# Decode attention on one core: uneven first output weights, one store semaphore, a split last weight load and smaller last value pieces

## The chip, the cores and the metric

The kernel runs on one core of a Trainium2 chip. The metric is the device time of one execution in microseconds (us). Three runs of the kernel before gave 1368.85, 1369.17 and 1373.74, a median of 1369.17 us.

## The reference

Two attention layers decode one token each for a batch of 4, and their outputs stand side by side.

```python
q = (x @ wq).reshape(B, Sq, Hq, Dh).transpose(0, 2, 1, 3)
scores = einsum("bhqd,bhkd->bhqk", q, k) * Dh ** -0.5
p = softmax(scores)
o = einsum("bhqk,bhkd->bhqd", p, v)
return o.transpose(0, 2, 1, 3).reshape(B, Sq, Hq * Dh) @ wo
```

Layer A has 32 query heads on 8 key heads and looks at the last 2048 of 8192 positions. Layer B has 32 heads with keys and values of their own over all 8192 positions. A head has 128 elements, a token 512; all arrays are bfloat16. The caches of B alone are 2 x 268 MB, and each byte is used once: nearly all of the work is reading.

## The kernel before, in words

**Chunks.** The work is cut into 40 chunks. Eight belong to A (one key head, all four batch rows; 2 MB of keys, 2 MB of values), 32 to B (four heads of one batch row; 8.39 MB of keys and as much of values). In SBUF each of the 128 partitions holds a row of consecutive positions, so that a load has 128 long rows.

**Queues.** SP issues all loads but the two small ones of x, in a fixed order (lines 468 to 489): A's weights, A's chunks with A's output weights (`dma_wo`, line 359) between them, then for B, before every fourth chunk, 512 rows of output weights (`dma_wos`, line 367), and for each chunk its keys (`dma_kB`, line 388) and its values (`dma_vB`, line 438). The last two loads of A's output weights (LATEWO = 2) come at the very end, behind B's last values. Each issue waits on semaphores for the moment at which its place in SBUF is free; as a rule that is some us before the queue has run dry.

**Pieces.** A chunk of B comes whole, or near the beginning and the end in pieces: the list in line 32 (LASTV) gives those of the last value chunk in tiles of 128 positions, of which a chunk has 256. GpSimd waits for each piece and passes its arrival on by raising a semaphore (`land_vB`, line 452, `land_wos`, line 461; emitted at line 82), in groups of eight tiles; the list QV in line 35 says before which groups TensorE waits.

**Compute.** TensorE transposes the keys (line 571), multiplies them with the query (line 613), and multiplies values with probabilities (`emit_pv`, line 747). It reorders B's output weights with matmuls (`reorder`, line 834), whose first reader of a load stands at the head of a chunk. `emit_fin` (line 852) multiplies a chunk's result with its output weights and adds it into one PSUM tile, `fin`: four products (one for each matrix row of the four that a partition holds) in two halves, which run side by side as a pair.

**The end.** After the last chunk's `emit_fin` TensorE ends B's sum (line 1041), does A's chunk 6, then waits for the last output weights and does A's chunk 7. `emit_out` (line 872) casts B's and A's sums with VectorE and stores each from ACT and from SP, four rows of 512 bytes each. SP waits for the stores at lines 1051 and 1052.

Every operation passes through a scheduler (`_Sched`, line 60) that gives each keyed operation a semaphore and a count; matmuls are recorded at lines 501 and 503 for all callers.

Of the kernel before, what the change touches and what calls it, by code (L numbers as in the profile page):

```python
# [13 lines left out]
P = 128  # L14
# [3 lines left out]
NH = 10  # L18
NWO = 2
LATEWO = 2  # L20
NPB = 2
NSM = 2
SLAG = 2
# [5 lines left out]
QUARTERS = (64, 64, 64, 64)  # L29
NLATE = 4  # L30
NEXTV = (128, 64, 64)
LASTV = (128, 64, 32, 32)
QK = (0, 4, 8)
QC = (16, 24)
QV = (0, 8, 16, 24, 28)
NBUSY = 2
MOREBUSY = 5
FILL = (6, 3)
# [140 lines left out]
def bass_concat_heads__sliding_block_cached__mha_block_cached__decode_kernel(  # L179
# [6 lines left out]
    DO = A_wo.shape[1]  # L186
# [23 lines left out]
    NCA = Hkv  # L210
# [9 lines left out]
    chunks.append(dict(chunks[NCA]))  # L220
    assert all(sum(x) == NTB for x in (LASTV, NEXTV, ENDK, QUARTERS, HALVES, WHOLE)) and NTA * 16 == 1024 and NTB * 4 == 1024
    NCP = (NTB - KMAIN) // TG

    sch = _Sched()
    with ExitStack() as es:
        block = es.enter_context(nc.Block())

        def sb(name, shape, dt):
            return es.enter_context(nc.sbuf_tensor(name, shape, dt))

        def ps(name, shape, dt):
            return es.enter_context(nc.psum_tensor(name, shape, dt))
# [3 lines left out]
        wos = sb("wos", [P, 4, DO], BF16)  # L236
# [29 lines left out]
        pm = sb("pm", [P, HB, NB, 4], F32)  # L266
        pbt = {0: sb("pba", [P, NPB, NTA * 16 + NW], BF16), 1: sb("pbb", [P, 2, NTB * 2 + NW], BF16)}
        oT = sb("oT", [P, NSM, 16], BF16)
# [12 lines left out]
        fin = ps("fin", [P, 512], F32)  # L281
        xtps = ms[:, XT0:XT0 + KC * NB].bitcast(BF16)
        po2 = tr[:, 2, :].bitcast(F32)

        semnames = ["eng_pe", "eng_dve", "eng_act", "eng_pool", "eng_sp", "d_x0", "d_x1", "d_o0", "d_o1", "r_k", "r_v", "r_c", "r_w"]
        semnames += ["d_h%d" % i for i in range(NH)] + ["d_%s%d_%d" % (f, n, i) for f in "kv" for n in range(1, 6) for i in range(n)]
        semnames += ["d_wo%d" % i for i in range(NWO)] + ["d_wos"]
        sems = {n: es.enter_context(nc.semaphore(n)) for n in semnames}
# [4 lines left out]
            out=identb[:, :], in_=onesb[:, :], pattern=[[1, P]], compare_op=ALU.is_equal,  # L293
# [4 lines left out]
            out=identf[:, :], in_=onesf[:, :], pattern=[[1, P]], compare_op=ALU.is_equal,  # L298
# [3 lines left out]
            out=ind[:, :].rearrange("u (x i) -> u x i", x=4), in_=onesf[0:4, :].rearrange("u (x i) -> u x i", x=4),  # L302
            pattern=[[1, 4], [0, P // 4]], compare_op=ALU.is_equal, fill=0.0, base=0, channel_multiplier=-1),
            waits=["c_onesf", "c_identf"], key="c_ind")
# [14 lines left out]
        for r in range(4):  # L319
            sch.add("pool", lambda e, r=r: e.affine_select(  # L320
                out=sel4[:, r, :], in_=onesb[:, :], pattern=[[0, 4], [-4, 32]], compare_op=ALU.is_equal,
# [4 lines left out]
        for u in range(4):  # L326
            sch.add("pool", lambda e, u=u: e.affine_select(
                out=back[:, :, :], in_=back[:, :, :], pattern=[[1, 4], [-1, P]], compare_op=ALU.not_equal,
# [21 lines left out]
        def dma_wq(ab, at):  # L350

            waits = take(("wq", ab), at, 2, ("qmm", ab))
            src = WQ[ab].rearrange("(p r) n -> p (r n)", r=KC)
            sch.add_dma("sp", lambda e: e.dma_start(flat(at, 2), src), "d_h%d" % at, waits=waits, key=("wq", ab))

        def wo_slot(g):
            return g % 2

        def dma_wo(g):

            src = A_wo[g * 4 * P:(g + 1) * 4 * P, :].rearrange("(p r) n -> p (r n)", r=4)
            slot = wo_slot(g)
            dst = wor[:, slot, :]
            sch.add_dma("sp", lambda e: e.dma_start(dst, src), "d_wo%d" % slot,
                        waits=[("fin", g - 2)] if g >= 2 else [], key=("wo", g))

        def dma_wos(hq):


            src = B_wo[4 * hq * P:4 * (hq + 1) * P, :].rearrange("(p r) n -> p (r n)", r=4)  # L370
            sch.add_dma("sp", lambda e: e.dma_start(wos[:, :, :].rearrange("p r n -> p (r n)"), src), "d_wos",
                        waits=[("reord", NCA + 4 * hq - 1, 3)] if hq else [], key=("wos", hq))

        def dma_A(kind, c):
            ch = chunks[c]
# [9 lines left out]
        def vpieces(c):  # L385
            return LASTV if c == NC - 1 else NEXTV if c == NC - 2 else HALVES if c <= NCA + 2 or c == NC - 3 else WHOLE

# [50 lines left out]
        def dma_vB(c):  # L438

            ch = chunks[c]  # L440
            src = B_v[ch["b"], 4 * ch["hq"]:4 * ch["hq"] + 4].rearrange("u (pp j) d -> (u pp) (j d)", pp=P // 4)
            dst = flat(VB, 4)
            pieces = vpieces(c)
            fam = "d_v%d_" % len(pieces)
            j0 = 0
            for i, n in enumerate(pieces):
                waits = held[4] + held[5] + held[6] + held[7] if c == NCA else [("pv", c - 1, 0 if j0 + n <= NTB // 2 else 1)]
                x = slice(j0 * P, (j0 + n) * P)
                sch.add_dma("sp", lambda e, x=x: e.dma_start(dst[:, x], src[:, x]), fam + str(i), waits=waits, key=("v", c, i))
                j0 += n  # L450

        def land_vB(c):
# [3 lines left out]
            for i, m in enumerate(pieces):  # L456
                sch.relay("pool", sems, "r_v", m // TG, [("v", c, i)])
            for g, end in zip(QV, QV[1:] + (NTB // TG,)):
                sch.tk[("vr", c, g)] = ("r_v", n * (NTB // TG) + end)
# [12 lines left out]
        for c in range(NCA):  # L472
            if c != 1 and c < NCA - 1:
                dma_A("k", c + 1)
            dma_A("v", c)
            if c == 2:
                dma_wq(1, 6)
            if c != 1 and c < NCA - LATEWO:
                dma_wo(c)
            if c == 0:  # L480
                dma_wo(1)
                dma_A("k", 2)
        for c in range(NCA, NC):
# [3 lines left out]
            dma_vB(c)  # L487
        for c in range(NCA - LATEWO, NCA):
            dma_wo(c)
# [9 lines left out]
        def pe_mm(o, l, r, start=True, stop=True, transpose=False, waits=(), key=None):  # L499
            if transpose:  # L500
                sch.add("pe", lambda e: e.transpose(o, l, r), waits, key)  # L501
            else:
                sch.add("pe", lambda e: e.matmul(o, l, r, start=start, stop=stop), waits, key)  # L503
# [223 lines left out]
        def spread_A(c, bs):  # L727

            for b in bs:
                sch.add("act", lambda e, b=b: e.activation(  # L730
                    probs_of(c).rearrange("p j (b c) -> p j b c", b=NB)[:, :, b, :], eA[:, c % 2, :].rearrange("p (j c) -> p j c", c=REP),
                    ACTF.Copy, scale=mk[:, b:b + 1]),
                    waits=[("exp1", c), "mk", ("c_pb", 0)] + ([("pv", c - NPB)] if c >= NPB else []) if b == 0 else [],
                    key=("exp", c) if b == NB - 1 else None)
# [12 lines left out]
        def emit_pv(c, g):  # L747
# [3 lines left out]
            for t in range(TG):  # L751
# [11 lines left out]
                if j == 0:  # L763
                    po_read[:] = []
                waits += [("vr", c, g)] if t == 0 and g in QV else []
                o = (po2 if h else po)[:, 0:NW]
# [85 lines left out]
        def emit_fin(c):  # L852
            ab = 0 if c < NCA else 1
            if ab == 1:
                ov = oz[:, :].rearrange("p (b u) -> p b u", b=NB)
                ops = [(ov[:, :, u], wol[:, u, :]) for u in range(4)]
                waits = ["c_oz", ("oT", c)]
            else:
                w = wor[:, wo_slot(c), :].rearrange("p (r n) -> p r n", r=4)
                ops = [(zA[:, c % 2, r * NB:(r + 1) * NB], w[:, r, :]) for r in range(4)]  # L860
                waits = [("z", c), ("wo", c)]

            for i, (l, r) in enumerate(ops):
                for h, (p0, x) in enumerate(out_halves(ab)):
                    pe_mm(fin[p0:p0 + NB, 0:DO // 2], l, r[:, x], start=False,
                          stop=i == len(ops) - 1 and c == NCA - 1, waits=waits if i == h == 0 else [],
                          key=("fin", c) if i == len(ops) - 1 and h == 1 else None)

        def out_halves(ab):
            return [(64 * (1 - ab) + 32 * h, slice(h * DO // 2, (h + 1) * DO // 2)) for h in (0, 1)]  # L870

        def emit_out(c):
            ab = 0 if c < NCA else 1
            at = out_halves(ab)
            rows = slice(at[0][0], at[1][0] + NB)
            sch.add("dve", lambda e: e.tensor_copy(outsb[rows, :], fin[rows, 0:DO // 2]), waits=[("end", 32) if ab else ("fin", c)], key=("osb", ab))
            for h, (p0, x) in enumerate(at):
                sch.add_dma("sp" if h else "act", lambda e, x=x, p0=p0: e.dma_start(out[:, 0, ab * DO + x.start:ab * DO + x.stop], outsb[p0:p0 + NB, :]),
                            "d_o%d" % h, waits=[("osb", ab)], key=("out", ab, h))


        A_ORDER = {1: ['gmax-1'], 2: ['bc-1', 'shift-1'], 3: ['exp-1'], 5: ['sums-1', 'sel-2'], 6: ['spread-1'], 7: ['norm-1', 'fin-2']}
# [78 lines left out]
        def whole_B(c):  # L961
# [26 lines left out]
            for g in range(ch["NG"]):  # L988
# [12 lines left out]
                if g == ch["NG"] - 2:  # L1001
                    add_first(c)
            norm_out(c)
            emit_fin(c)

        def finish_A():
# [33 lines left out]
        for p0, x in out_halves(1):  # L1040
            pe_mm(fin[p0:p0 + NB, 0:DO // 2], zz[:, :], sel4[:, 0:2, :].rearrange("p r x -> p (r x)"), start=False, key=("end", p0))
        for c in range(NCA - LATEWO, NCA - 1):
            emit_fin(c)
        emit_out(NC - 1)
        emit_fin(NCA - 1)
        emit_out(NCA - 1)

        @block.sync
        def _(e):
            sch.emit("sp", e, sems)  # L1050
            e.wait_ge(sems["d_o0"], 32)
            e.wait_ge(sems["d_o1"], 32)

        def loop_on(eng, slots):

# [50 lines left out]
```

## Time and profile before

| | |
|---|---|
| median of three runs | 1369.17 us |
| the profiled execution | 1368.99 us |
| its span, first to last instruction | 1367.3 us |
| TensorE (PE) busy | 1222.9 us, 89% |
| VectorE (DVE) busy | 731.9 us, 54% |
| ScalarE (ACT) busy | 555.0 us, 41% |
| GpSimd (POOL) busy | 202.8 us, 15% |
| read from HBM | 587.21 MB |
| granted TensorE clock, mean | 0.976 |

The profile is one execution. Its span is the time between the first and the last instruction on the core; 1.69 us of the execution lie outside it. All windows and start times below are us from the span's start. "DMA share" is the mean busy share of the core's sixteen DMA engines by the time that their packets took, each packet being counted in the window in which it starts, so a window can show slightly more than 1. A row of the chain of waits that names a DMA has the time of its issue and the time until it landed. In a row of the timeline the first number is the start, the second the time from the first start to the last end of the instructions merged in it.

### The profile page before, as it was taken

The numbers are of one execution on the slowest core, as the hardware profiler recorded it, in microseconds if no ns is written. First come the engines' busy times: TensorE is split into PE (matmuls) and PEld (weight loads), VectorE is DVE, ScalarE is ACT, GpSimd is POOL, SyncE is SP. The second block draws the span as 40 slices with busy tenths as digits, with TensorE's granted clock in tenths as the row PEclk, the third lists the DMA queues.
The fourth block names the chain that finished last, engine by engine and source line by source line (L and its number), as shares of the span: only waits on it lengthen the run. The fifth ranks groups of instructions, "written<-read, shape, count | busy, mean of one in ns | idle before, by whom it ended". The sixth has DMA issues, their size and how long they took to land.

```text
span 1367.3 us, 62934 instructions
## 1 busy us (share of the span) xinstructions
PE 1222.9 (89%) x27807; PEld 1126.6 (82%) x27843; DVE 731.9 (54%) x1495; ACT 555.0 (41%) x777; POOL 202.8 (15%) x84
## 2 busy tenths in 40 slices
PE   6688799989898999888989899889899898899998
PEld 5687698878887988888889888878898888888888
DVE  2575455545455555554555555545555555455565
ACT  2453344434344443333444344334444343344443
POOL 2000022222210222222101222221012222200000
PEclk9998999999999999999999999999999999999999
DMA  9999999999999999999999999999999999999998
GB/s 398 428 427 431 432 438 431 428 435 424 441 431 429 431 429 437 435 432 429 437 430 437 429 429 431 439 433 429 429 439 435 429 430 437 439 428 429 429 427 372
DMA packets 16629, 587.52 MB, mean 430 GB/s; under 512 B 1864, under 2 KB 1888, under 8 KB 3936
## 3 DMA queue, kind: packets, MB, share of 16 engines
q1 hardware_dynamic: 16576, 587.21, 99.7%
q8 instruction: 15, 0.25, 0.1%
q14 instruction: 6, 0.05, 0.0%
q10 hardware_dynamic: 32, 0.01, 0.0%
HBM read 587.21 MB, written 0.01 MB: 429 GB/s over the span
## 4 chain that ended last, share of the span: by engine, by line
DMA 57%; PE 38%; issue 2%; DVE 2%; ACT 1%; SPq 0%; ACTq 0%; POOLq 0%; DVEq 0%
DMA kv<-in_B_k_cache_dram 51%; PE tr L501 22%; PE sc L503 10%; DMA kv<-in_A_k_cache_dram 4%; PE tr L503 3%; DMA kv<-in_B_v_cache_dram 2%; PE po L503 2%; PE ms L503 1%; PE fin L503 0%; DVE kt L578 0%; DVE sA L631 0%; ACT pbb L700 0%; PE sc L933 0%; ACT pba L730 0%; PE ms L501 0%
## 5 line engine op out<-in xcount | busy, mean ns | idle before, releaser
L501 PE MATMUL tr<-identb,kv 128*128 128x128 bf16 x8704 | 672.1, 223 | 48.5 <-POOLq L82 35.7
L578 DVE COPY kt<-tr 128x1024 bf16<-128x1024 bf16 x736 | 502.8, 691 | 320.3 <-PE tr L501 317.1
L501 PEld LDWEIGHTS tr<-identb,kv 128*128 128x128 bf16 x8704 | 520.9, 100 | 60.3 <-issue 52.0
L576 ACT ACTIVATE kt<-tr 128x1024 bf16<-128x1024 bf16 x352 | 359.3, 1023 | 455.4 <-PE tr L501 453.2
L503 PE MATMUL sc<-qq,kt 128*128 128x64 bf16 x8192 | 401.1, 192 | 11.1 <-DVE kt L578 9.4
L503 PEld LDWEIGHTS sc<-qq,kt 128*128 128x128 bf16 x8192 | 330.7, 98 | 17.7 <-DVE kt L578 12.7
L425 POOL COPY kv<-kv 128x4096 int32<-128x4096 int32 x54 | 193.0, 3602 | 988.4 <-DMA kv<-in_B_k_cache_dram 988.4
L700 ACT ACTIVATE pbb<-sc,negb 32x128 bf16<-32x128 f32 x256 | 137.9, 539 | 134.3 <-DVE negb L682 131.5
L503 PE MATMUL tr<-pbb,kv 128*128 128x64 bf16 x4096 | 135.8, 193 | 28.1 <-ACT pbb L700 25.5
L503 PEld LDWEIGHTS tr<-pbb,kv 128*128 128x128 bf16 x4096 | 131.1, 99 | 31.9 <-issue 29.7
L503 PE MATMUL po<-pbb,kv 128*128 128x64 bf16 x4096 | 135.0, 194 | 4.3 <-issue 4.3
L503 PEld LDWEIGHTS po<-pbb,kv 128*128 128x128 bf16 x4096 | 127.5, 98 | 5.4 <-issue 4.4
L848 ACT ACTIVATE wol<-tr 128x512 bf16<-128x512 f32 x32 | 19.1, 597 | 203.4 <-PE po L503 203.4
L850 DVE CAST wol<-tr 128x512 bf16<-128x512 f32 x64 | 41.2, 686 | 54.8 <-PE tr L503 54.8
L933 PE MATMUL sc<-sel,identb 128*128 128x512 bf16 x167 | 51.1, 384 | 13.6 <-issue 13.6
L933 PEld LDWEIGHTS sc<-sel,identb 128*128 128x128 bf16 x167 | 16.2, 97 | 48.6 <-issue 38.5
L707 DVE TENSOR_REDUCE rs<-pbb 128x4 f32<-128x512 bf16 x32 | 22.0, 687 | 50.1 <-ACT pbb L700 50.1
L780 DVE RECIPROCAL ib<-ms 128x8 f32<-128x8 f32 x32 | 6.6, 208 | 58.1 <-PE ms L503 58.1
L503 PE MATMUL tr<-wos,back 32*128 32x512 bf16 x384 | 34.8, 383 | 0.6 <-issue 0.5
L503 PE MATMUL po<-wos,back 32*128 32x512 bf16 x128 | 33.9, 384 | 0.0
L668 DVE TENSOR_REDUCE gm<-ms 4x4 f32<-4x128 f32 x72 | 19.8, 275 | 23.3 <-PE ms L501 23.3
L648 DVE TENSOR_REDUCE rh<-sc 128x4 f32<-128x512 f32 x32 | 22.1, 692 | 14.3 <-PE sc L503 14.3
(92 smaller groups left out, 506.2 us busy)
## 6 DMA issues: line engine op xcount, KB each, us to landing
kv<-in_B_v_cache_dram SPq DMA_DIRECT2D x10, 4096.0 KB, 24.1
kv<-in_B_k_cache_dram SPq DMA_DIRECT2D x7, 4096.0 KB, 19.7
kv<-in_A_k_cache_dram SPq DMA_DIRECT2D x8, 2048.0 KB, 15.8
kv<-in_A_v_cache_dram SPq DMA_DIRECT2D x8, 2048.0 KB, 16.7
kv<-in_B_k_cache_dram SPq DMA_DIRECT2D x6, 2048.0 KB, 26.2
kv<-in_B_v_cache_dram SPq DMA_DIRECT2D x3, 2048.0 KB, 29.9
kv<-in_A_wq_dram SPq DMA_DIRECT2D x1, 4096.0 KB, 12.5
wor<-in_A_wo_dram SPq DMA_DIRECT2D x8, 512.0 KB, 21.2
```

Source lines behind the costliest of these rows:

```text
L425: sch.add("pool", lambda e, dst=dst, org=org: e.tensor_copy(dst, org), waits=[("T", s0 + ch["NG"] - 1)] if g == QC[0] else [])
L501: sch.add("pe", lambda e: e.transpose(o, l, r), waits, key)
L503: sch.add("pe", lambda e: e.matmul(o, l, r, start=start, stop=stop), waits, key)
L576: sch.add("act", lambda e: e.activation(dst, src, ACTF.Copy), waits=waits, key=("ev", s))
L578: sch.add("dve", lambda e: e.tensor_copy(dst, src), waits=waits, key=("ev", s))
L648: sch.add("dve", lambda e: e.tensor_reduce(out=dst, in_=src, axis=AX.X, op=ALU.max), waits=[("S", ch["s"] + (half + 1) * ch["NG"] // 2 - 1 ...
L668: sch.add("dve", lambda e: e.tensor_reduce(out=gm[0:C, m, 0:U], in_=src, axis=AX.X, op=ALU.max), waits=[key_of("trm", c, half)], key=key_o ...
L700: sch.add("act", lambda e, src=src, dst=dst, pp=pp, u=u: e.activation(dst, src, ACTF.Exp, bias=negb[pp, half, u:u + 1], scale=scale), wait ...
L707: sch.add("dve", lambda e: e.tensor_reduce(out=dst, in_=probs_of(c, half).rearrange("p j u -> p u j"), axis=AX.X, op=ALU.add), waits=[("ex ...
L848: sch.add("act", lambda e, u=u, o=o: e.activation(wol[:, u, :], o, ACTF.Copy), waits=[("reord", c, u)], key=("wol", c, u))
L850: sch.add("dve", lambda e, u=u, o=o: e.tensor_copy(wol[:, u, :], o), waits=[("reord", c, u)], key=("wol", c, u))
L933: return e.matmul(sc[:, 1, :], identb[:, :], sel4[:, :, :].rearrange("p r x -> p (r x)"), start=True, stop=True)
```

## The change

Four things are edited. The first load of B's output weights (`dma_wos`, hq = 0) becomes three loads of 64, 51 and 13 partitions on the same semaphore; its key is the third. The last load of A's output weights becomes two: the first three of the four matrix rows that each partition holds, and the fourth; the fourth pair of A's last products waits for the second load. The four stores share one semaphore, and SP waits once for 64. The last value chunk's pieces are 128, 64, 48 and 16 tiles in place of 128, 64, 32 and 32, and TensorE's last wait in a value chunk moves from group 28 to group 30.

```diff
+LASTWO = 3
+UNEVEN = (64, 51, 13)
...
-LASTV = (128, 64, 32, 32)
+LASTV = (128, 64, 48, 16)
...
-QV = (0, 8, 16, 24, 28)
+QV = (0, 8, 16, 24, 30)
...
+            if g == NCA - 1:
+                for h, x in enumerate((slice(0, LASTWO * DO), slice(LASTWO * DO, 4 * DO))):
+                    sch.add_dma("sp", lambda e, x=x: e.dma_start(dst[:, x], src[:, x]), "d_wos" if h else "d_wo%d" % slot,
+                                waits=[] if h else [("fin", g - 2)], key=("wo", g, h))
+                return
...
+            if hq == 0:
+                rows = 0
+                for n in UNEVEN:
+                    x = slice(rows, rows + n)
+                    rows += n
+                    sch.add_dma("sp", lambda e, x=x: e.dma_start(dst[x, :], src[x, :]), "d_wos", key=("wos", hq) if rows == P else None)
+                return
...
-                waits = [("z", c), ("wo", c)]
+                waits = [("z", c), ("wo", c, 0) if c == NCA - 1 else ("wo", c)]
...
-                          stop=i == len(ops) - 1 and c == NCA - 1, waits=waits if i == h == 0 else [],
+                          stop=i == len(ops) - 1 and c == NCA - 1,
+                          waits=waits if i == h == 0 else [("wo", c, 1)] if c == NCA - 1 and (i, h) == (LASTWO, 0) else [],
...
-                            "d_o%d" % h, waits=[("osb", ab)], key=("out", ab, h))
+                            "d_out", waits=[("osb", ab)], key=("out", ab, h))
...
-            e.wait_ge(sems["d_o0"], 32)
-            e.wait_ge(sems["d_o1"], 32)
+            e.wait_ge(sems["d_out"], 64)
```

More of the change, by code (lines that the diff above doesn't have):

```diff
@@ L283, in bass_concat_heads__sliding_block_cached__mha_block_cached__decode_kernel @@
         po2 = tr[:, 2, :].bitcast(F32)
-        semnames = ["eng_pe", "eng_dve", "eng_act", "eng_pool", "eng_sp", "d_x0", "d_x1", "d_o0", "d_o1", "r_k", "r_v", "r_c", "r_w"]
+        semnames = ["eng_pe", "eng_dve", "eng_act", "eng_pool", "eng_sp", "d_x0", "d_x1", "d_out", "r_k", "r_v", "r_c", "r_w"]
         semnames += ["d_h%d" % i for i in range(NH)] + ["d_%s%d_%d" % (f, n, i) for f in "kv" for n in range(1, 6) for i in range(n)]
@@ L370, in dma_wos @@
             src = B_wo[4 * hq * P:4 * (hq + 1) * P, :].rearrange("(p r) n -> p (r n)", r=4)
-            sch.add_dma("sp", lambda e: e.dma_start(wos[:, :, :].rearrange("p r n -> p (r n)"), src), "d_wos",
-                        waits=[("reord", NCA + 4 * hq - 1, 3)] if hq else [], key=("wos", hq))
+            dst = wos[:, :, :].rearrange("p r n -> p (r n)")
+            waits = [("reord", NCA + 4 * hq - 1, 3)] if hq else []
+            if hq == 0:
[5 more added lines that the diff above has]
+                return
+            sch.add_dma("sp", lambda e: e.dma_start(dst, src), "d_wos", waits=waits, key=("wos", hq))
         def dma_A(kind, c):
```

## The prediction

> **What bounds the kernel now.** I read the page's slices first, then the list of DMA queues, then the chain that ended last in order of time.
>
> ```profile
> PE   6688799989898999888989899889899898899998
> DMA  9999999999999999999999999999999999999998
> q1 hardware_dynamic: 16576, 587.21, 99.7%
> q10 hardware_dynamic: 32, 0.01, 0.0%
> HBM read 587.21 MB, written 0.01 MB: 429 GB/s over the span
> ```
>
> The sixteen DMA engines are busy in every slice but the last; TensorE isn't. SP's queue alone takes 99.7% of their time. The chain of waits shows that this is a rate and not a latency:
>
> ```profile
> 573.26 27.82 DMA kv<-in_B_k_cache_dram
> 611.71 28.08 DMA kv<-in_B_k_cache_dram
> 651.96 26.52 DMA kv<-in_B_k_cache_dram
> 689.24 27.95 DMA kv<-in_B_k_cache_dram
> 727.81 29.36 DMA kv<-in_B_k_cache_dram
> ```
>
> Columns: issue, time to landing. Issue plus time gives landings at 601.08, 639.79, 678.48, 717.19 and 757.17. The issues wander by 3 us, the landings are 38.71, 38.69 and 38.71 apart: one key and one value chunk, each of 4 x 8192 x 128 x 2 B = 8.39 MB, at 433.6 GB/s. The last gap is 39.98 because 0.52 MB of output weights lie in it. So nothing on a compute engine in the middle of the kernel counts. What counts is when the slowest DMA engine ends and what follows the last bytes.
>
> ```profile
> core 0: us, PE busy (x) PEld busy (x) DVE busy (x) ACT busy (x) POOL busy (x), PEclk, DMA share, GB/s
> 1361.20:1362.40 1.20, 0.51 (x18) 0.51 (x19) 0.00 (x0) 0.00 (x0) 0.00 (x0) 1.00 1.03 423
> 1362.40:1362.80 0.40, 0.40 (x15) 0.40 (x12) 0.00 (x0) 0.00 (x0) 0.00 (x0) 1.00 0.88 358
> 1362.80:1363.20 0.40, 0.40 (x10) 0.29 (x9) 0.00 (x0) 0.00 (x0) 0.00 (x0) 1.00 0.46 184
> 1363.20:1363.60 0.40, 0.13 (x5) 0.09 (x5) 0.17 (x1) 0.00 (x0) 0.00 (x0) 1.00 0.08 31
> 1363.60:1364.00 0.40, 0.40 (x14) 0.34 (x12) 0.00 (x0) 0.00 (x0) 0.00 (x0) 1.00 0.03 10
> ```
>
> The DMA share falls in steps: the engines don't end together. In 1363.20 to 1363.60 about one works (0.08 of 16), in the next window one for half of it (0.03 x 0.40 x 16 = 0.19 us), so the last ends near 1363.79. From 1362.40 on the shares add up to 0.40 x (0.88 + 0.46 + 0.08 + 0.03) = 0.58 us for each engine: equal engines would end at 1362.98. The last is 0.81 us behind the mean, and no engine is more than 1.39 us ahead of it. These 0.81 us are all that moving bytes between engines can win.
>
> **The change part by part.** First the uneven output weights. It adds no bytes. How rows are dealt to engines can be read from the counts above: q10 holds the four DMAs of four rows that ACT issues (two loads, two stores) and has 32 packets, 8 each: four rows and four completions, so four engines with a row each. With 115 loads of 128 rows and SP's two stores, 115 x (128 + 16) + 2 x 8 = 16576 is q1's count exactly: sixteen engines of eight rows. Both are equal shares. If equal shares are the rule, 64 rows are four on each of 16 engines, 51 = 3 x 17 can only be 17 rows on each of three (or all on one), and 13 are single rows on thirteen. Three engines then carry 4 + 17 + 1 = 22 rows in place of 8, ten carry 5, three carry 4.
>
> The Trainium skill, page "DMA: Bandwidth & Descriptors", section "Why a DMA increments its semaphore by 16 and not by 1", states such a rule: the largest number up to 16 that divides the slowest dimension, on the lowest-numbered engines, so 3 for 51 rows and 13 for 13. The trace agrees for 4 and 128 rows; no row shows 51.
>
> A row of 4 KB at 429/16 = 26.8 GB/s takes 0.153 us. So the three get 14 x 0.153 = 2.14 us more, the others 3 or 4 rows less: 0.46 or 0.61 us. If the engine that ends last is one of the thirteen, and the three don't overtake it, the end comes 0.46 to 0.61 earlier; I take **-0.46**, ten of the thirteen having that.
>
> Would the three not overtake? By the end rows alone they would, as 2.14 + 0.46 = 2.60 is more than the 1.39 us that any engine is ahead. But a lead at the end needn't be the lead at 110 us, when these rows pass, because leads are lost on the way:
>
> ```profile
> 181.86 28.16 DMA kv<-in_B_k_cache_dram
> 222.16 26.63 DMA kv<-in_B_k_cache_dram
> 244.10 0.33 SPq L449 DMA_DIRECT2D kv<-in_B_v_cache_dram  x1
> ```
>
> The key chunk lands at 222.16 + 26.63 = 248.79 on its last engine, and the next load is issued at 244.10: the last engine has 4.7 us left, an engine 4.7 ahead has nothing. The very first load shows what an issue costs on top: SP issues it at 0.8 and no DMA works before 1.84.
>
> ```profile
> 0.80 0.42 SPq L354 DMA_DIRECT2D kv<-in_A_wq_dram  x1
> 0.00:1.84 1.84, 0.00 (x0) 0.00 (x0) 0.00 (x0) 0.14 (x1) 1.15 (x8) 1.00 0.00 1
> ```
>
> So an engine over 4.7 - 1.0 = 3.7 us ahead must wait there, and what it waits is given away. If the three stand that far ahead, the added 2.14 us fill their waiting. No row names the engines; this is where I choose, and the rivals hold the other side.
>
> What else the split issues: two more DMAs on SP ahead of B's first keys.
>
> ```profile
> 99.11 0.54 SPq L380 DMA_DIRECT2D kv<-in_A_v_cache_dram  x1
> 99.69 0.59 SPq L371 DMA_DIRECT2D wos<-in_B_wo_dram  x1
> 100.33 6.30 SPq L410 DMA_DIRECT2D kv<-in_B_k_cache_dram  x3
> wos<-in_B_wo_dram SPq DMA_DIRECT2D x8, 512.0 KB, 23.9
> DMA to landing us min/median/max: 11.7/23.9/24.7
> L503 PEld LDWEIGHTS tr<-wos,back x384: 90/92/146, 121.4 to 1328.2; 32*128 32x128 bf16 x192
> ```
>
> Two issues of 0.59 us delay the keys' issue by 1.2. (The fifth and sixth rows are from the view of the tile wos.) The weights land 11.7 us after their issue at the earliest, so the queue covers this ten times. Their first reader starts at 121.4; from 99.69 + 11.7 = 111.4 there are 10 us for a landing up to 2.14 later (without that cover, TensorE would start B up to 2.14 late). In the queue one more DMA costs at most 39.98 - 38.70 - 0.52 MB / 433.6 GB/s (1.21) = 0.07 us beyond its bytes; three more (one below) cost 0 to 0.21; I take **+0.10**.
>
> Now the tail:
>
> ```profile
> 1327.74 34.05 DMA kv<-in_B_v_cache_dram
> 1361.89 0.87 PE L503 MATMUL tr<-pbb,kv 128*128 128x64 bf16 x24 [1.14 <-POOLq L82]
> 1362.60 0.36 PE L503 MATMUL tr<-t,identf 128*128 128x4 f32 x2
> 1362.83 0.39 PE L503 MATMUL tr<-pbb,kv 128*128 128x64 bf16 x8
> 1363.49 0.60 PE L503 MATMUL fin<-wol,oz 128*4 128x256 bf16 x8 [0.27 <-DVE oz L814]
> 1363.98 0.96 PE L503 MATMUL fin<-wor,zA 128*4 128x256 bf16 x14
> 1364.99 0.43 DVE L876 CAST outsb<-fin 36x256 bf16<-36x256 f32 x1 [0.30 <-PE fin L503]
> DMA to landing us min/median/max: 9.1/21.2/35.5
> ```
>
> The last value piece lands at 1327.74 + 34.05 = 1361.79 and starts four groups of eight products, (0.87 - 0.19)/23 = 0.029 us apart (0.19 is one's own length). With pieces of 48 and 16 the third lands 0.52 MB earlier, 1.22 us at 429 GB/s, so at 1360.67 in TensorE's time; its six groups take 48 x 0.029 = 1.41 and end at 1362.08. That is after the last landing, so TensorE is late next, and two groups are left. Before, the same place (16 of 24 done) was at 1361.89 + 0.47 = 1362.36: **0.28** earlier.
>
> This alone would win nothing. The eight products of the last output weights run in pairs 0.109 us apart ((0.60 - 0.27)/3); with the end at 1364.94 their first pair starts at 1364.94 - 0.27 - 3 x 0.109 = 1364.34. Those weights land 35.5 us after an issue near 1328.7 (the largest of the eight, last row, from the view of the tile wor), at 1364.2, and the previous pair left room at 1364.31. Two paths meet there within 0.03 us. The split (the last output weights as three matrix rows and one) lets three pairs start when three quarters are in, 0.13 MB or 0.31 us sooner: at the later of 1364.31 - 0.28 and 1364.34 - 0.31, both 1364.03; they end at 1364.36, the fourth pair waits for 1364.34. It starts at 1364.36 in place of 1364.67: **-0.31** for the cast, the stores and the end. Behind the added wait stand only that pair and the cast. If a wait or a smaller packet ate all of it, the tail would give 0; more than 0.33 it can't give, since the last landing holds.
>
> One semaphore for four stores: SP now waits once.
>
> ```profile
> SPq L878 <- DVE outsb L876: 35.9, 2, 35.6
> SPq L1052 <- DMA out_dram<-outsb: 1.0, 1, 1.0
> ```
>
> The 1.0 us is the store's own landing, which stays; the second wait follows it at once. 0 to 0.1; I take 0.
>
> The Trainium skill, same page, section "Rules for kernel authors", advises against cutting a transfer by partitions, as all parts share the same engines and one transfer of 128 does. By it the cut at 64, 51 and 13 would bring nothing; that is the second rival's time.
>
> **Sum**: -0.46 + 0.10 - 0.31 = -0.67 on the profiled execution's own 1368.99 (span 1367.3 and 1.69 around it) is 1368.32. The median of the three runs is 0.18 above the profiled one, so 1368.5.
>
> **The rivals.** (1) *The three loaded engines become the last*, slower than before. If the three stand at the greatest lead of the end rows, they end 2.14 - 1.39 = 0.75 after today's last one: 1369.17 + 0.75 + 0.10 - 0.31 = 1369.7. If today's last is one of the three (3 in 16 by chance), 2.14 count: 1371.1. It decides from a lead of 2.14 us at 110 us downward; above a lead of 2.60 the forecast holds whole. For it: the 1.39 at the end; against it: leads are cut at 244.10, so the end shows only what is left. (2) *The cut doesn't shift rows*: the 51 rows go to all engines after all. Then only tail and added DMAs count: 1369.17 - 0.31 + 0.10 = 1369.0. (3) Anything larger, such as a stalled queue at 110 us: over 1376.
>
> **How the numbers follow.** Forecast 0.55 (1368.5; 1368.2 to 1368.9 with the bounds of its terms), rival 1 0.28, rival 2 0.12, rest 0.05. Half of rival 1 lies below 1370.0. The runs shown differ by 0.3 us at the low end (1368.85, 1369.17), so the range is 1367.7 to 1370.0, which leaves out 0.14 + 0.05. A measurement of this kernel can tell about 0.5%, 6.8 us, from no change; every case but the rest lies inside: faster 0.01, same 0.95, slower 0.04.
>
> **What would show it.** Right: the DMA share in the last 2 us falls more steeply and ends near 1363.4; the last products of the value groups come as 16 after the last wait, and the last fin pair starts about 0.3 after three others without a gap; the landings in mid-kernel keep 38.70. Wrong: a flat foot of about three engines (share 0.19) for 0.7 us or more at the end is rival 1; the same foot as before, one engine for 0.6 us, is rival 2; a gap in TensorE at 121 us is the lost cover.

## The result, and the profile after

The changed kernel takes 1371.75 us (median of 22 runs, 1371.22 to 1377.14), the kernel before 1368.94 (22 runs): 2.8 us more, ratio 1.0022 [1.0016, 1.0028]. That is within 0.5%, as forecast, but slower, and above the forecast range of 1367.7 to 1370.0. The profiled execution took 1371.73 us, with a span of 1370.0.

Two lines of the page of the changed kernel: the rate in 40 slices, and SP's queue (packets, MB, share).

```profile
GB/s 399 427 428 392 438 429 434 436 431 425 434 432 434 431 432 444 417 440 434 440 431 427 444 431 429 429 444 429 429 429 444 429 429 436 436 429 428 431 428 367
q1 hardware_dynamic: 16736, 587.21, 99.7%
```

The bytes are the same. The packets are 160 more than the 16576 of before. The second load of A's last output weights adds 144 of them (128 rows and 16 completions), which leaves 16 for the cut at 64, 51 and 13: (64 + 16) + (51 + 3) + (13 + 13) = 160 in place of 128 + 16. So 51 rows went to three engines, as the forecast had it; on sixteen engines they would have had 16 completions. (The kernel with the cut alone, e1 below, has 16592 packets, the same 16 more.) But the fourth slice has a hole: 392 GB/s between 428 and 438. A slice is 34 us, so some 40 GB/s less are 1.4 MB.

The windows view of the changed kernel, microsecond by microsecond (the last two columns are DMA share and GB/s), finds the place:

```profile
103.00:107.00 4.00, 4.00 (x91) 3.67 (x88) 3.28 (x10) 3.69 (x7) 0.00 (x0) 1.00 1.03 438
107.00:108.00 1.00, 0.72 (x26) 0.69 (x25) 0.41 (x2) 0.26 (x1) 0.00 (x0) 1.00 1.03 356
108.00:109.00 1.00, 1.00 (x41) 1.00 (x38) 0.53 (x2) 0.00 (x0) 0.00 (x0) 1.00 1.09 274
109.00:110.00 1.00, 1.00 (x42) 1.00 (x39) 0.93 (x3) 0.00 (x0) 0.00 (x0) 1.00 0.99 238
110.00:111.00 1.00, 0.39 (x16) 0.30 (x12) 0.96 (x2) 0.00 (x0) 0.00 (x0) 1.00 0.93 197
111.00:112.00 1.00, 0.46 (x8) 0.27 (x9) 0.76 (x5) 0.00 (x0) 0.00 (x0) 1.00 1.14 270
112.00:113.00 1.00, 0.48 (x16) 0.39 (x13) 0.74 (x5) 0.00 (x0) 0.00 (x0) 1.00 1.20 258
113.00:114.00 1.00, 1.00 (x34) 0.98 (x35) 0.59 (x2) 0.05 (x1) 0.00 (x0) 1.00 1.00 254
114.00:115.00 1.00, 1.00 (x44) 1.00 (x42) 0.56 (x2) 0.97 (x3) 0.00 (x0) 0.63 0.74 283
```

The same stretch of the kernel before, in one window:

```profile
107.00:114.00 7.00, 5.05 (x153) 4.42 (x147) 5.00 (x17) 0.47 (x2) 0.00 (x0) 1.00 1.02 428
```

When the cut weights pass, the engines stay busy (share about 1) and move about 60% as much: each packet takes longer. The trace has the time of every packet, and the views above only sum them up. A row of 4 KB of these weights took 0.28 us on average (0.16 before), and the rows of 16 KB of the other loads that start in this stretch took 1.01 us (0.62 before). From 107 to 114 us, (428 - 264) GB/s x 7 us = 1.15 MB are missing (264 is the mean of the seven rows). The weights themselves are 0.52 MB, so the loads beside them are slow too. The chain of waits shows what is left of that later, first for the changed kernel, then in two lines for the kernel before:

```profile
224.24 26.61 DMA kv<-in_B_k_cache_dram
...
927.62 26.54 DMA kv<-in_B_k_cache_dram
...
964.89 27.97 DMA kv<-in_B_k_cache_dram
...
1082.17 28.07 DMA kv<-in_B_k_cache_dram
...
1122.41 27.20 DMA kv<-in_B_k_cache_dram
...
1330.15 33.28 DMA kv<-in_B_v_cache_dram
```

```profile
1081.50 26.55 DMA kv<-in_B_k_cache_dram
...
1118.85 27.91 DMA kv<-in_B_k_cache_dram
```

The key chunk that landed at 248.79 before lands at 250.85, 2.06 later. From there to 1110 us little is added: 954.16 and 992.86 are 38.70 apart, as before. But then 1110.24 and 1149.61 are 39.37 apart, against 38.71 before (1108.05 and 1146.76): another 0.66 us. The packets show what happens there. One single engine falls 0.66 back, in this kernel and in the kernel before. Before, that engine has more than this to spare; in the changed kernel it is the last one, so the landing waits for it. What holds it up isn't shown. The end windows of the changed kernel:

```profile
1364.80:1365.20 0.40, 0.40 (x20) 0.40 (x17) 0.11 (x1) 0.00 (x0) 0.00 (x0) 1.00 0.91 356
1365.20:1365.60 0.40, 0.40 (x14) 0.40 (x11) 0.00 (x0) 0.00 (x0) 0.00 (x0) 1.00 0.66 238
1365.60:1366.00 0.40, 0.40 (x10) 0.28 (x9) 0.00 (x0) 0.00 (x0) 0.00 (x0) 1.00 0.19 67
1366.00:1366.40 0.40, 0.13 (x5) 0.11 (x6) 0.17 (x1) 0.00 (x0) 0.00 (x0) 1.00 0.06 23
1366.40:1366.80 0.40, 0.40 (x14) 0.33 (x12) 0.00 (x0) 0.00 (x0) 0.00 (x0) 1.00 0.06 20
1366.80:1367.20 0.40, 0.40 (x15) 0.32 (x9) 0.15 (x1) 0.00 (x0) 0.00 (x0) 1.00 0.00 0
```

Read as the prediction read them: three engines work in 1365.60 to 1366.00 (0.19 x 16 = 3.0), then one for 0.8 us. By the packets, fifteen engines are done by 1365.80 and one at 1366.75: it is one engine that is late, not three. The mean engine ends at 1364.80 + 0.40 x (0.91 + 0.66 + 0.19 + 0.06 + 0.06) = 1365.55, the last at 1366.40 + 0.06 x 0.40 x 16 = 1366.78. Before it was 1362.98 and 1363.79. So the mean moved by 2.57 us, and the last fell back from 0.81 to 1.23 behind the mean.

### The profile page after: what moved, and what is told of

The parts are those of the page before. It is cut to its first block, busy times and chain, and to the rows that moved or that the text cites. A ratio compares the mean times of both kernels' runs of the same rounds, so it can differ in the third digit from the quotient of the medians.

```text
span 1370.0 us, 62936 instructions
## 1 busy us (share of the span) xinstructions
PE 1222.5 (89%) x27807; PEld 1126.5 (82%) x27843; DVE 731.9 (53%) x1495; ACT 555.5 (41%) x777; POOL 203.0 (15%) x84
## 4 chain that ended last, share of the span: by engine, by line
DMA 58%; PE 38%; issue 2%; DVE 2%; ACT 1%; SPq 0%; ACTq 0%; POOLq 0%; DVEq 0%
DMA kv<-in_B_k_cache_dram 52%; PE tr L516 22%; PE sc L518 10%; DMA kv<-in_A_k_cache_dram 4%; PE tr L518 3%; DMA kv<-in_B_v_cache_dram 2%; PE po L518 1%; PE ms L518 1%; PE fin L518 0%; DVE sA L646 0%; PE sc L949 0%; DVE kt L593 0%; ACT pbb L715 0%; ACT pba L745 0%; PE ms L516 0%
## 5 line engine op out<-in xcount | busy, mean ns | idle before, releaser
L865 DVE CAST wol<-tr 128x512 bf16<-128x512 f32 x64 | 41.2, 686 | 54.9 <-PE tr L518 54.9
```

The source lines that it names most:

```text
L865: sch.add("dve", lambda e, u=u, o=o: e.tensor_copy(wol[:, u, :], o), waits=[("reord", c, u)], key=("wol", c, u))
```

## The experiments

**Theories.** P: a load that covers only some partitions, in neighbouring rows, lets several DMA engines write into the same part of SBUF, and everything that flows beside it is held up. T (rival 1 of the prediction): the three engines with 22 rows end last. I: it is the number of loads, or their one semaphore. Later S: the rows read from HBM decide, not the partitions written. All kernels but the first keep the other edits of the change (tail, store semaphore), so the one to compare with is e2_rest. All times are medians of 11 runs, with the ratio to the kernel before (1368.85 to 1368.90 beside these kernels), but e5 (5 runs) and e11 (12).

| kernel, first weights as | us | ratio | GB/s 107 to 114 us | key chunk lands |
|---|---|---|---|---|
| before: 128 rows | 1368.9 | | 428 | 248.79 |
| e1: 64, 51, 13, nothing else changed | 1372.07 | 1.0021 [1.0012, 1.0030] | 273 | 251.09 |
| e2: 128 rows, the rest of the change | 1368.69 | 0.9997 [0.9988, 1.0006] | 421 | 248.77 |
| e3: 64, 64 | 1371.09 | 1.0016 [1.0007, 1.0025] | 276 | 250.78 |
| e4: 128 rows in three column parts | 1368.87 | 1.0001 [0.9992, 1.0010] | 412 | 248.77 |
| e5: 64, 64 for all eight loads | 1389.88 | 1.0159 [1.0142, 1.0175] | 297 | 250.74 |
| e6: 64 even rows, 64 odd rows | 1368.67 | 1.0002 [0.9993, 1.0011] | 421 | 248.55 |
| e7: eight loads of 16 | 1371.11 | 1.0016 [1.0007, 1.0025] | 267 | 251.23 |
| e8: written as e3, read as e6 | 1371.72 | 1.0021 [1.0012, 1.0030] | 286 | 250.98 |
| e9: 64 even, 51 odd, 13 odd rows | 1370.42 | 1.0009 [1.0000, 1.0018] | 309 | 249.86 |
| e10: e2 with other last value pieces | 1368.72 | 0.9996 [0.9988, 1.0005] | 421 | 248.57 |
| e11: 112, 16 | 1371.09 | 1.0019 [1.0010, 1.0027] | 295 | 250.70 |

**e1_uneven_only**: the kernel before with the cut alone.

```diff
+UNEVEN = (64, 51, 13)
...
+                for n in UNEVEN:
+                    x = slice(rows, rows + n)
+                    rows += n
+                    sch.add_dma("sp", lambda e, x=x: e.dma_start(dst[x, :], src[x, :]), "d_wos", key=("wos", hq) if rows == P else None)
```

> The kernel before with the uneven first output weights alone (64, 51 and 13 rows). All theories here are about these loads, so all expect nearly the whole loss of the change, and somewhat more, since the tail edits are missing: 2.5 to 3.2 us slower than before, with the GB/s of all loads down to 200 to 280 between 107 and 114 us while the DMA share stays near 1. If it comes out within 0.5 us of before, the loss lies in the tail edits and all theories fall.

The cut alone costs 3.2 us: it is the whole loss.

**e2_rest**: the change without the cut.

```diff
-            if hq == 0:
...
-                return
             sch.add_dma("sp", lambda e: e.dma_start(dst, src), "d_wos", waits=waits, key=("wos", hq))
```

> The changed kernel with the first output weights as one load of 128 rows again; tail edits and the one semaphore stay. All theories: no dip at 107 to 114 us, 0.1 to 0.4 us faster than before. Over 1 us slower than before would mean that the tail edits cost.

0.2 us faster by the medians, with an interval of -1.6 to +0.8 us. Its TensorE timeline and its end windows:

```profile
1360.48 0.41 PE L510 MATMUL tr<-pbb,kv 128*128 128x64 bf16 x8 [1.29 <-POOLq L84]
1360.72 0.37 PE L510 MATMUL ms<-rsb,onesf 128*128 128x12 f32 x2
1360.94 1.56 PE L510 MATMUL tr<-pbb,kv 128*128 128x64 bf16 x48
1362.34 0.36 PE L510 MATMUL tr<-t,identf 128*128 128x4 f32 x2
...
1363.72 0.93 PE L510 MATMUL fin<-wor,zA 128*4 128x256 bf16 x14
```

```profile
1362.40:1362.80 0.40, 0.40 (x14) 0.40 (x10) 0.00 (x0) 0.00 (x0) 0.00 (x0) 1.00 0.87 335
1362.80:1363.20 0.40, 0.16 (x6) 0.03 (x2) 0.18 (x1) 0.00 (x0) 0.00 (x0) 1.00 0.60 218
1363.20:1363.60 0.40, 0.38 (x8) 0.32 (x11) 0.00 (x0) 0.00 (x0) 0.00 (x0) 1.00 0.19 67
1363.60:1364.00 0.40, 0.40 (x16) 0.34 (x12) 0.00 (x0) 0.00 (x0) 0.00 (x0) 1.00 0.01 3
```

The value groups now run through without a wait for the last piece, and in this execution A's last products end at 1364.65, against 1364.94 before. But behind the first eight products stands the row sum (ms<-rsb), which holds the groups up by 1360.94 - 1360.72 = 0.22 us. The mean engine ends at 1362.40 + 0.40 x (0.87 + 0.60 + 0.19 + 0.01) = 1363.07, the last at 1363.66, 0.59 behind. The share of 0.19 stands here too, so this foot of about three engines isn't made by the cut.

**e3_halves** and **e4_columns**: equal shares for all engines, first by rows, then by columns. The first diff is e3's, the second e4's.

```diff
-UNEVEN = (64, 51, 13)
+UNEVEN = (64, 64)
```

```diff
-UNEVEN = (64, 51, 13)
+UNEVEN = (1024, 816, 208)
...
-                    sch.add_dma("sp", lambda e, x=x: e.dma_start(dst[x, :], src[x, :]), "d_wos", key=("wos", hq) if rows == P else None)
+                    sch.add_dma("sp", lambda e, x=x: e.dma_start(dst[:, x], src[:, x]), "d_wos", key=("wos", hq) if rows == 4 * DO else None)
```

> The changed kernel with 64 and 64 rows in place of 64, 51 and 13: the same bytes, every DMA engine gets four and four rows, none is loaded more. Theory T (three engines with 22 rows trail, and the loads behind them wait): like the kernel without the uneven cut, 0.1 to 0.4 us faster than before, no dip. Theory P (a load that covers only a part of the partitions lets several engines write into the same part of SBUF, and the loads that flow beside it are held up too): slower than before by 1 to 2.5 us, with a dip of the GB/s to 200 to 300 for 3 to 7 us.

> The changed kernel with the first output weights as three loads of all 128 rows, cut by columns (1024, 816 and 208 of 2048 elements): the same three issues, one semaphore, nearly the same bytes for each load, but even on partitions and engines. Theories T and P: no dip, 0.0 to 0.4 us faster than before. Theory I (it is the number of loads or the shared semaphore that costs): 2 us or more slower than before, as the change.

Halves cost 2.4 us against e2 with no engine loaded more than another, so T isn't the main part. Three loads with three completions on the same semaphore cost 0.2 at most when each covers all partitions, so I falls. The windows of e3, then of e4:

```profile
107.00:114.00 7.00, 5.05 (x158) 4.65 (x157) 4.91 (x17) 0.31 (x2) 0.00 (x0) 1.00 0.99 276
```

```profile
107.00:114.00 7.00, 5.05 (x153) 4.58 (x152) 4.98 (x17) 0.31 (x1) 0.00 (x0) 0.96 1.01 412
```

**e5_halves_all**: if the cost belongs to the cut, eight cuts pay it eight times.

```diff
-UNEVEN = (64, 51, 13)
+UNEVEN = (64, 64)
...
-            if hq == 0:
-                rows = 0
-                for n in UNEVEN:
+            rows = 0
+            for n in UNEVEN:
```

> All eight loads of B's output weights as 64 and 64 rows (the changed kernel else). Cut so, the first load alone cost 2.2 us against the kernel before. Theory P gives a price for each load, wherever it stands: 8 x 2.0 = 16, so 12 to 18 us slower than before, with eight dips. Rival: the price is one of the place (the passage from A to B, where A's loads flow beside): then 1.5 to 4 us slower, one dip.

21.0 us more than before by the median, above the 12 to 18 expected, and 14.8 in the profiled run (1383.83 against 1368.99): 1.9 to 2.6 for each of eight cuts. In that run's chain six later gaps with weights in them are 41.2 to 42.5 us long in place of 40.0, so the price is paid wherever the cut load stands. The runs lie far apart (1383.83 to 1393.36), so the size for one cut is taken from e3.

**e6_even_odd**: the same count, rows and engines' shares as e3, but each load spreads over all partitions.

```diff
+UNEVEN = (0, 1)
...
+                    x = slice(n, P, 2)
```

> The first output weights as the 64 even rows and the 64 odd rows (two loads, each reaching from the first partition to the last). Theory P in its narrow form (what counts is how much of SBUF's partitions the load spans, since half of them can be written at half the rate only): no dip below 350 GB/s, 0.4 us faster to 0.5 us slower than before. Rival: any load of fewer than 128 partitions costs, or any that deals rows to engines in another way than the loads beside it: 1.5 to 2.5 us slower, as the halves.

Nothing is lost, in the time or in the window of e6:

```profile
107.00:114.00 7.00, 5.04 (x157) 4.65 (x156) 4.90 (x17) 0.30 (x2) 0.00 (x0) 0.98 1.00 421
```

**e7_sixteens**: by P, sixteen engines on 16 neighbouring partitions should collide worse than on 64.

```diff
+UNEVEN = (16, 16, 16, 16, 16, 16, 16, 16)
```

> The first output weights as eight loads of 16 rows that follow each other. Theory P by dose: 16 neighbouring partitions are a smaller part of SBUF than 64, so the rate while they flow falls below the 220 to 280 GB/s of the halves, to 100 to 180, and the loss grows to 3 to 6 us. Rival (the cost is one of cutting by rows, whatever the span): about the halves' 2.2 us plus at most 0.07 for each of six more loads.

The same as the halves, 1371.11, with 267 GB/s. The dose doesn't count; the expectation of P for it missed.

```profile
107.00:114.00 7.00, 5.05 (x155) 4.53 (x152) 5.00 (x17) 0.37 (x1) 0.00 (x0) 1.00 1.01 267
```

**e8_half_dst**: halves of the partitions, fed with even and odd source rows. It puts rows of these weights into other partitions than the reference, so B's part of the output is another one; bytes and loads are those of e3.

```diff
+                    x, y = slice(n * 64, n * 64 + 64), slice(n, P, 2)
+                    sch.add_dma("sp", lambda e, x=x, y=y: e.dma_start(dst[x, :], src[y, :]), "d_wos", key=("wos", hq) if n else None)
```

> The first output weights as two loads of 64 neighbouring partitions, the first fed with the even rows of the source and the second with the odd ones. This puts rows of these weights in the wrong partitions, so a part of B's output differs; work and bytes are the same. Theory P (the side that is written decides): as the halves, 1.5 to 2.7 us slower than before. Rival S (the side that is read decides: 64 neighbouring rows are one stretch of 256 KB of HBM): like one whole load, within 0.5 us of before.

As slow as e3, so the side that is written decides, and S falls. Its window:

```profile
107.00:114.00 7.00, 5.05 (x152) 4.44 (x147) 5.00 (x17) 0.46 (x2) 0.00 (x0) 0.97 1.01 286
```

**e9_uneven_odd**: the uneven deal (22, 5 and 4 rows) with rows spread as in e6.

```diff
+UNEVEN = ((0, 64), (1, 51), (103, 13))
...
+                for r, n in UNEVEN:
+                    x = slice(r, r + 2 * n - 1, 2)
```

> The first output weights as 64 even rows, 51 odd rows and the last 13 odd rows: the uneven deal over the DMA engines (17 rows on three engines, if dealt in equal shares) without neighbouring partitions, so without the dip that theory P prices. What is left is the deal alone. Rival 1 of the prediction (the three loaded engines become the last): 0.3 to 1.0 us slower than the kernel with the tail edits alone (1368.69), so 1369.0 to 1369.7. The prediction's step (the last engine sheds three or four rows): 0.3 to 0.6 us faster than it, so 1368.1 to 1368.4. No dip below 330 GB/s in either case; if a dip of the halves' size comes back, a load of 51 rows has a cost of its own.

1.7 us slower than e2, more than expected, and with a dip below the 330 GB/s that was expected at the least. Window and end of e9:

```profile
107.00:114.00 7.00, 5.15 (x161) 4.77 (x162) 4.78 (x17) 0.30 (x2) 0.00 (x0) 1.00 1.00 309
...
1363.60:1364.00 0.40, 0.40 (x21) 0.40 (x17) 0.01 (x1) 0.00 (x0) 0.00 (x0) 1.00 0.71 284
1364.00:1364.40 0.40, 0.40 (x15) 0.40 (x12) 0.00 (x0) 0.00 (x0) 0.00 (x0) 1.00 0.69 254
1364.40:1364.80 0.40, 0.30 (x9) 0.18 (x7) 0.06 (x1) 0.00 (x0) 0.00 (x0) 1.00 0.28 100
1364.80:1365.20 0.40, 0.23 (x6) 0.19 (x8) 0.12 (x1) 0.00 (x0) 0.00 (x0) 1.00 0.06 23
1365.20:1365.60 0.40, 0.40 (x16) 0.34 (x12) 0.00 (x0) 0.00 (x0) 0.00 (x0) 1.00 0.04 15
```

One engine ends last here (0.06 x 16 = 1.0 from 1364.80 on): the last at 1365.20 + 0.04 x 0.40 x 16 = 1365.46, the mean at 1363.60 + 0.40 x (0.71 + 0.69 + 0.28 + 0.06 + 0.04) = 1364.31, so 1.15 behind in place of 0.59 in e2. That is 0.56, and 0.50 of it comes late, as in the changed kernel: its key chunks at 1109.13 and 1148.34 are 39.21 apart, 0.50 more than before. The kernel also has a hole of its own (309 GB/s; the key chunk lands 1.1 late): odd rows cut into 51 and 13 slow the stream too, and which of the two loads does it isn't tested. So the price of the deal without any slowing, T alone, isn't measured by itself.

**e10_tail_40_24**: e2 with last value pieces that leave TensorE less to do between the last two landings.

```diff
-LASTV = (128, 64, 48, 16)
+LASTV = (128, 64, 40, 24)
-QV = (0, 8, 16, 24, 30)
+QV = (0, 8, 16, 24, 29)
```

> The kernel with the tail edits alone, and the last value pieces as 128, 64, 40 and 24 tiles. In the trace of the tail edits with 48 and 16, TensorE was still at the piece of 48 (with the product for the row sums in it) 0.69 us after the last landing. With 40 and 24 it is through when the last piece lands, and 24 tiles then take 0.10 + 16 x 0.029 = 0.57 to the same place: 0.1 us faster than with 48 and 16, so about 1368.6 (0.3 faster than before), if the last output weights don't hold it. Rival: they do, and the time is that of 48 and 16.

No difference from e2 (1368.72 against 1368.69). No version here is measurably faster than the kernel before.

**e11_112_16**: is it how few partitions a load spans? 112 of 128 span nearly all.

```diff
+UNEVEN = (112, 16)
```

> The first output weights as 112 and 16 neighbouring rows (the changed kernel else); each DMA engine gets seven rows and one. Narrow theory P (the span counts): 112 rows span nearly all, the 16 are an eighth of the bytes, so 0.1 to 0.7 us slower than with one load (1368.69). Wider rival (any cut into neighbouring rows that moves the boundaries between engines): 1.5 to 2.5 us slower, as the halves, with their dip.

1371.09, as the halves, with 295 GB/s. So the span isn't it either, and the narrow form of P missed again (0.1 to 0.7 us expected).

```profile
107.00:114.00 7.00, 5.05 (x158) 4.65 (x157) 4.91 (x17) 0.30 (x2) 0.00 (x0) 1.00 1.02 295
```

What holds for all of these: weights whose neighbouring rows are dealt to the sixteen engines in other shares than eight each cost 2.4 us against e2 (e3, e7, e11; 3.0 in e8), whatever the sizes. The same weights cut by columns, or by even and odd rows, cost nothing that can be measured. P stands in this wider form. The packets show how the other loads are held up: each row of 16 KB that starts between 109 and 111 us takes 0.88 to 1.39 us in e3 and 1.01 to 1.13 in e7, in place of 0.61 to 0.63 before and in e6. That the written side decides is shown (e8 against e6); that it is engines meeting at the same part of SBUF is argued from it.

**What stays open** is which engine meets which. No view here shows it, and the trace's packets carry no number of an engine. The Trainium skill, page "SBUF — State Buffer", section "Door 1: The DMA port swizzle (why `[64,N]` ≈ `[32,N]`)", says that DMA bandwidth depends on how many of 16 ports the partitions reach, and that 64 neighbouring partitions reach eight, for about 218 GB/s. The 0.52 MB would take 2.4 us in place of 1.2 by it, 1.2 more, as an estimate from that page; e3 shows 2.4 more. For 16 partitions it has four ports and about 109 GB/s, so 3.6 us more in e7 by the same estimate, which shows the same 2.4 as e3; and 112 partitions reach all ports by its port table, so that only the 16 rows behind them are short of ports, but e11 pays 2.4 as well. So the trace agrees with the direction for halves and not with the sizes.

## Why the prediction was wrong, point by point

**What bounds the kernel: right.** The gaps between landings that the chain shows in mid-kernel keep 38.70, all but one (39.37 between 1110 and 1150), and what was lost at 110 us is still there at the end.

**The uneven weights: wrong, and this is the step that failed.** The deal was right (51 rows on three engines, by the packet count). The price was not: forecast -0.46, measured +3.06 (1371.75 against 1368.69 of e2). The prediction took 0.153 us for a row of 4 KB from the mean rate and let it hold for any load: "It adds no bytes". In the changed kernel such a row took 0.28 us, and the 16 KB rows of the loads beside it 1.01 in place of 0.62: the rate fell to 264 GB/s for 7 us, on all loads in flight. Halves alone, with equal shares, lose 2.4 us that way. No rival had this; rival 3 named a stalled queue at 110 us but priced it over 1376.

The choice "If the three stand that far ahead, the added 2.14 us fill their waiting" didn't hold either. Before, the sixteen engines ended the last load that landed whole ahead of the weights between 102.44 and 104.79, by its completion packets, so none had the lead of 2.60 above which "the forecast holds whole". After the cut weights, in the load that ended from 115.96 to 119.42, three engines came in 1.2 to 1.5 us behind the other thirteen, as rival 1 had it. But that isn't what is left later. The key chunk lands at 250.85, as in e3 with its equal shares (250.78), and the late foot is one engine for 0.8 us, not rival 1's three for 0.7 us or more. What the changed kernel loses beyond e3 is 0.66 by the medians (1371.75 - 1371.09). That is as much as the one engine loses between 1110 and 1150. Whether that engine is one of the three, and so whether the uneven deal cost these 0.66 us, stays open; e8, with equal shares, stands at 1371.72 too. So the time fell past rival 1's 1369.7 to 1371.1, mainly by another cause.

**Three more DMAs, +0.10: not contradicted.** e4 has the two that the cut adds with all partitions each and stands 0.2 above e2, with intervals wider than that.

**The tail, -0.31: not decided by the times.** e2 gives -0.2 with an interval that includes zero. In its profile the last products do end 0.29 earlier. One part of the working was wrong: "its six groups take 48 x 0.029 = 1.41" left out the row sum of 0.22 us among them, so TensorE is later at the last landing than forecast, and part of the 0.29 is how that execution's loads landed (the third piece was read at 1360.48, the forecast had 1360.67).

**The rest: right.** The cover held: SP's issues moved (by less than the 1.2 us forecast), and the first reader didn't wait. The timeline of SP, then of TensorE, of the changed kernel:

```profile
99.48 1.52 SPq L385 DMA_DIRECT2D wos<-in_B_wo_dram  x3
101.04 5.38 SPq L425 DMA_DIRECT2D kv<-in_B_k_cache_dram  x3
```

```profile
121.25 0.63 PE L518 MATMUL tr<-wos,back 32*128 32x512 bf16 x3 [0.50 <-issue]
```

The keys are issued 0.71 later than before, and the weights' first reader starts at 121.25 with the same 0.50 us of issue before it (121.46 before). One semaphore for the stores saved nothing, as forecast; SP's wait in the changed kernel:

```profile
SPq L227 <- DMA out_dram<-outsb: 1.1, 1, 1.1
```

## What to carry to other kernels

In a kernel that the DMA rate bounds, a load cut into groups of neighbouring partitions isn't free even when bytes, engines and queue stay the same: here each such cut of 0.52 MB cost about 2 to 3 us, taken from all loads in flight, and the windows' GB/s beside a DMA share of 1 is where it shows. Where a load must be cut, cut it by columns so that each part still covers all 128 partitions. Bytes moved between engines should be priced by an experiment and not by the mean rate of a row: here the row itself took 0.28 us in place of the 0.153 reckoned with.

## What the runs showed of the hardware

- Sixteen busy engines can move 197 to 274 GB/s instead of 428: from 108 to 114 us of the changed kernel the DMA share stays at 0.93 to 1.20. A share near 1 is no proof of the full rate.
- The size of the parts of neighbouring rows hardly counts (64 and 64, 8 x 16, 112 and 16: 1371.09 to 1371.11), the written partitions do (e8 against e6: 3.0 us for the same source rows).
- The Trainium skill, page "DMA: Bandwidth & Descriptors", section "Rules for kernel authors", says of two transfers to disjoint halves of the partitions: don't bother, they serialize on the same engines. The runs show more than that: for neighbouring halves a loss of 2.4 us (e3 against e2), for even and odd halves none (e6).
- A cut into three loads that each cover all partitions cost 0.2 us by the medians while the queue had work waiting (e4 against e2), with intervals of about 1.2 us either way.
